# First token tiles loaded in two halves on two queues, first gate slice moved to the other queue, mask sum moved behind the prologue

## The chip, the cores and the metric

One core of one Trainium2 chip. The metric is the device time of one execution in microseconds (us). It was taken over several executions ("runs") of each kernel, with those of the kernel before interleaved on the same chip. The profiler gives a trace of one of the runs of each kernel. In its lines PE is TensorE, DVE is VectorE and ACT is ScalarE; L427 is line 427 of that kernel. A load "lands" when its last part has been reported; "pace" is the time from one matmul's start to the next.

## The reference

`x` has 2048 tokens of 512 values in bf16. It is normalised, then goes through a linear-attention block with 32 heads and through a gated block; both results are added to `x`:

```python
xn = (x - mean(x)) / sqrt(var(x) + 1e-5)
q, k, v = split(xn @ wqkv)                     # 512 x 1536
phi(t)  = concat(softmax(t @ w_phi), softmax(-t @ w_phi))
o       = phi(q) @ (phi(k).T @ v) / (phi(q) @ sum(phi(k)) + 1e-6)
out     = x + o @ wo + ((xn @ w_gate) * (xn @ w_up)) @ w_down     # 1792 wide inside
```

Only the first microseconds matter here: tokens come in 16 tiles of 128. The first four are centred, transposed on TensorE, and multiplied by the value weights `wv` (four blocks q = 0 to 3 of 128 x 512) and by the first slices of `w_gate` and `w_up`.

## The kernel before

The kernel is a list of steps with declared reads and writes. A small scheduler puts them in an order for each engine; between `sc.pin = True` and `sc.pin = False` the order is the one written. A DMA names the engine whose queue issues it: SP ("the first queue") or ACT ("the second queue"). The parts that the change touches:

```python
def load_x(t0, n, eng=SP):                       # n tiles of 128 KB
    ...
    sc.dma(eng, lambda e: e.dma_start(o, i), [], [("x", t) for t in range(t0, t0 + n)], n * 131072)

sc.pin = True
load_x(0, 1)                # first queue
load_x(1, 1, ACT)           # second queue
load_x(2, 1)
load_v(ACT, 1)              # value weights, 128 KB each
load_v(SP, 0)
load_v(ACT, 3)
load_v(SP, 2)
load_x(3, 1)
load_gu(SP, 0, (1,))        # up slice 0, 256 KB
act(sbf("lnv", 0, 1), eps_f, ["eps"], ["pace"])
load_gu(ACT, 0, (0,))       # gate slice 0, 256 KB, on the second queue
load_gu(SP, 1)              # gate and up slice 1, 384 KB each
# ... further weights and tiles on the first queue (cut)

# mask sum, early on VectorE:
dve(lambda e: e.tensor_reduce(out=epsz, in_=m1, axis=AX.XY, op=ALU.add), ["mask16"], ["epsz1"], 64)
dve(lambda e: e.tensor_scalar(out=epsz, in0=epsz, scalar1=1e-6, ...), ["epsz1"], ["epsz"], 1)
```

and the head of the pinned prologue, in the order that every engine keeps:

```python
warm(7)                       # seven matmuls of constants, 128 x 512
warm(1, 512, [("x", 0)])      # an eighth, when tile 0 has landed
sc.pin = True
ln_mean_split(0)              # half of the mean on ACT, half on VectorE
ln_mean_split(1)
ln_center_split(0)            # x - mean, in two halves of columns, on VectorE
ln_center_split(1)
x_transpose(0, 2, 0)          # PE
ln_mean_split(2)
x_transpose(0, 3, 1)
warm(1, 128)
x_transpose(1, 4, 0, DVE)
ln_center_whole(2)
x_transpose(1, 5, 1, DVE)
warm(1, 128)
for t in range(2):            # values of tiles 0 and 1 with weights q = 1, then q = 0
    v_matmul(t, t, ((1,), (0,)), stop=False)
x_transpose(2, 6, 0)
x_transpose(2, 4, 1, DVE)
for t in range(2):
    v_matmul(t, t, ((3,), (2,)), start=False)
# ... tile 3, gate and up products of slice 0 (cut)
```

The softmax here doesn't subtract the row's maximum and nothing guards it: scores larger than these inputs give would overflow.

## Time and profile before

| | before |
|---|---|
| median of the first 3 runs | 213.94 us (213.79 to 214.33) |
| span of the profiled run | 212.6 us |
| PE busy | 208.8 us, 98% |
| first transpose on PE | 4.78 us |
| PE without any stall from, to | 6.60 us, 209.7 us |

Two lines of the profile's page, the busy table and the chain of work that ended last by engine:

```profile
...
PE 208.8 (98%) x1476; PEld 125.6 (59%) x1476; DVE 165.8 (78%) x281; ACT 144.6 (68%) x350; POOL 108.8 (51%) x137
...
PE 97%; DMA 1%; DVE 1%; issue 0%
...
```

PE is the bound. A busy PE is not proof of it, since the ends of matmuls are modelled, so the starts were read as well: after 6.60 us they follow each other every 0.216 us (512 columns) or 0.109 us (256) to the last matmul. The time is therefore decided by when the prologue lets PE run freely.

The chain of waits in that prologue, in order of time (start us, us, what):

```profile
...
0.79 2.89 DMA arena<-in_A_x_dram
...
3.70 0.57 DVE arena L427 x3
...
4.38 0.08 DVE arena L427
4.46 0.27 DVE arena L434
...
4.78 0.65 PE ps L474 x4
...
6.07 1.12 PE ps L247 x4
...
```

The chain is a landing (issued at 0.79, landed at 3.68), VectorE work, then PE. VectorE's own timeline (start us, busy us, engine, line, operation, what ended the idle time before):

```profile
...
3.10 0.15 DVE L363 TENSOR_SCALAR arena<-arena 128x1 f32<-128x1 f32 x1
3.70 0.42 DVE L427 TENSOR_SCALAR_CACHE_REDUCE arena<-arena 128x256 bf16<-128x256 bf16 x1 [0.44 <-DMA arena<-in_A_x_dram]
...
4.04 0.41 DVE L427 TENSOR_SCALAR_CACHE_REDUCE arena<-arena 128x256 bf16<-128x256 bf16 x1
...
4.38 1.11 DVE L434 TENSOR_SCALAR arena<-arena 128x256 bf16<-128x256 bf16 x4
...
```

L427 are the means of tiles 0 and 1, L434 the four centring steps (two for each tile). The mask sum ends at 3.25, so VectorE sits idle for 0.44 us before tile 0 comes. Since the mean of tile 1 stands before the centring of tile 0, a late tile 1 would hold up tile 0 too. Here it does not: tile 1 landed at 3.84, while VectorE was still busy with tile 0.

PE's timeline in the same stretch:

```profile
...
4.78 0.65 PE L474 MATMUL ps<-arena 128*128 128x128 bf16 x4 [0.39 <-DVE arena L434]
...
5.33 0.63 PE L474 MATMUL ps<-arena 128*128 128x128 bf16 x4
...
5.87 1.33 PE L247 MATMUL ps<-arena 128*128 128x512 bf16 x4
7.03 0.39 PE L474 MATMUL ps<-arena 128*128 128x128 bf16 x4
...
```

L474 are the transposes, L247 the products. The first group of four 512-column products takes 1.33 us because PE still runs at half pace: their starts are 0.427 us apart until 6.3 us.

### The profile page before, as it was taken

The page shows a single profiled execution, that of the slowest core. Times are in us where ns is not written, and L with a number is a line of the kernel's source. Part 1 is how long each engine was busy: PE and PEld are TensorE (multiplying, and loading weights), DVE is VectorE, ACT ScalarE, POOL GpSimd, SP SyncE. Part 2 cuts the span into 40 slices and gives each one's busy share as a digit, 9 for nine tenths or more (in the row PEclk, how much of TensorE's full clock was granted, in tenths as well). Part 3 has the DMA queues.
Part 4 walks back from the last instruction along what each step waited for, and adds up shares of the span by engine and source line. Part 5 has one row for each costly group of instructions (what it writes and reads, how often), then busy time and mean ns, then how long its engine had stood idle before and what let it go on. Part 6 is the DMA issues. An engine that isn't in the chain of part 4 may idle for free.

```text
span 212.6 us, 4047 instructions
## 1 busy us (share of the span) xinstructions
PE 208.8 (98%) x1476; PEld 125.6 (59%) x1476; DVE 165.8 (78%) x281; ACT 144.6 (68%) x350; POOL 108.8 (51%) x137
## 2 busy tenths in 40 slices
PE   7999999999999999999999999999999999999995
PEld 2665444444554444444444444456888898899884
DVE  3686699998986647758989989896888898897622
ACT  4459998885989999987878977564544444432220
POOL 4030393243312448998895472204658549558540
DMA  5999119479500320331321223414265836556511
GB/s 166 305 283 372 65 35 187 89 200 328 104 3 0 49 49 3 60 59 33 72 53 26 49 52 49 104 54 65 48 80 131 190 70 135 125 128 148 123 49 49
DMA packets 49252, 22.29 MB, mean 105 GB/s; under 512 B 38097, under 2 KB 47697, under 8 KB 49233
## 3 DMA queue, kind: packets, MB, share of 16 engines
q1 hardware_dynamic: 48272, 21.39, 43.4%
q10 hardware_dynamic: 960, 0.66, 1.0%
q8 instruction: 11, 0.18, 0.4%
q14 instruction: 9, 0.07, 0.1%
HBM read 11.03 MB, written 2.10 MB: 62 GB/s over the span
## 4 chain that ended last, share of the span: by engine, by line
PE 97%; DMA 1%; DVE 1%; issue 0%
PE ps L247 91%; PE ps L553 2%; PE ps L611 2%; DMA arena<-in_A_x_dram 1%; PE ps L381 1%; PE ps L474 1%; DVE arena L427 0%; DVE arena L924 0%; DVE arena L434 0%; PE ps L1001 0%
## 5 line engine op out<-in xcount | busy, mean ns | idle before, releaser
L247 PE MATMUL ps<-arena 128*128 128x512 bf16 (+2 forms) x1160 | 200.0, 330 | 0.0
L247 PEld LDWEIGHTS ps<-arena 128*128 128x128 bf16 (+1 forms) x1160 | 110.9, 98 | 73.4 <-ACT arena L228 0.3
L228 ACT ACTIVATE arena<-ps 128x512 bf16<-128x512 f32 (+3 forms) x117 | 59.3, 538 | 17.9 <-PE ps L247 12.4
L228 ACT ACTIVATE arena<-arena 128x32 f32<-128x32 f32 (+8 forms) x131 | 52.4, 424 | 6.0 <-DVE arena L894 3.0
L894 DVE TENSOR_TENSOR arena<-ps,arena 128x512 f16<-128x512 f32 (+1 forms) x56 | 38.3, 685 | 19.5 <-ACT arena L228 14.2
L516 POOL TENSOR_TENSOR arena<-arena 128x1024 bf16<-128x1024 bf16 x16 | 31.0, 1934 | 38.0 <-ACT arena L228 38.0
L228 ACT ACTIVATE arena<-ps,arena 128x512 bf16<-128x512 f32 (+1 forms) x55 | 35.5, 671 | 10.1 <-PE ps L247 10.0
L506 DVE TENSOR_REDUCE arena<-arena 128x64 f32<-128x1024 bf16 x32 | 38.6, 1210 | 3.3 <-ACT arena L228 3.3
L855 POOL TENSOR_TENSOR arena<-arena 128x256 f16<-128x256 f16 x32 | 24.3, 768 | 13.0 <-DMA arena<-arena 11.7
L228 ACT ACTIVATE ps<-ps 128x256 f32<-128x256 f32 x24 | 8.8, 368 | 29.0 <-PE ps L247 29.0
L833 DVE TENSOR_TENSOR arena<-arena 128x896 f16<-128x896 f16 x32 | 23.7, 749 | 3.2 <-PE ps L247 3.1
L924 DVE SCALAR_TENSOR_TENSOR arena<-ps,arena 128x256 bf16<-128x256 f32 (+1 forms) x24 | 13.5, 569 | 10.4 <-PE ps L247 10.0
L773 POOL TENSOR_TENSOR arena<-arena 128x512 f16<-128x512 bf16 x14 | 16.2, 1175 | 4.7 <-DVE arena L894 3.3
L959 POOL TENSOR_TENSOR arena<-arena 128x512 f32<-128x512 f32 x8 | 9.5, 1192 | 17.1 <-ACT arena L228 17.1
L522 POOL TENSOR_TENSOR arena<-arena 128x512 bf16<-128x512 bf16 x16 | 17.2, 1074 | 0.9
L621 DVE TENSOR_TENSOR arena<-ps,arena 128x512 f16<-128x512 f32 x16 | 11.0, 687 | 1.4
L405 DVE BATCH_NORM_STATS2 arena<-arena 128x6 f32<-128x512 bf16 x16 | 10.4, 672 | 0.4 <-DMA arena<-in_A_x_dram 0.4
L520 POOL TENSOR_TENSOR arena<-arena 128x32 f32<-128x32 f32 x16 | 4.2, 266 | 9.5 <-ACT arena L228 9.5
L668 DVE BATCH_NORM_STATS2 arena<-arena 128x6 f32<-128x512 bf16 x14 | 9.0, 681 | 0.0
L553 PEld LDWEIGHTS ps<-arena 128*128 128x128 bf16 x128 | 6.0, 97 | 3.5
L802 DVE TENSOR_TENSOR arena<-arena 128x1792 f16<-128x1792 f16 (+1 forms) x8 | 7.0, 903 | 0.0
L611 PEld LDWEIGHTS ps<-arena 128*128 128x128 bf16 x128 | 6.2, 97 | 1.2
(54 smaller groups left out, 68.1 us busy)
## 6 DMA issues: line engine op xcount, KB each, us to landing
arena<-in_A_x_dram SPq DMA_DIRECT2D x8, 256.0 KB, 3.3
out_dram<-arena SPq DMA_DIRECT2D x15, 128.0 KB, 2.0
arena<-in_B_w_down_dram SPq DMA_DIRECT2D x1, 1792.0 KB, 7.9
arena<-in_A_x_dram SPq DMA_DIRECT2D x3, 512.0 KB, 4.2
arena<-arena SPq DMA_TRANSPOSE x44, 3.0
arena<-in_B_w_gate_dram SPq DMA_DIRECT2D x1, 640.0 KB, 8.7
arena<-in_B_w_up_dram SPq DMA_DIRECT2D x1, 640.0 KB, 9.9
arena<-in_B_w_gate_dram SPq DMA_DIRECT2D x1, 512.0 KB, 5.3
```

The lines of the kernel that those rows point to most:

```text
L228: return sc.step(ACT, lambda e: e.activation(out=out_ap, in_=in_ap, func=func, scale=scale, **kw), reads, writes, 130.0 + 0.833 * n)
L247: ins = e.matmul(out_ap, lhsT=l, rhs=r, start=start and i == 0, stop=stop and i == npair - 1, **kw)
L506: dve(lambda e: e.tensor_reduce(out=sm, in_=e_v, axis=AX.X, op=ALU.add), [(name, s, 0), (name, s, 1)], [("sums", sr)], 1024)
L516: pool(lambda e: e.tensor_tensor(out=e_w, in0=e_w, in1=r_w, op=ALU.mult), [(name, s, 0), (name, s, 1), ("rs", n)], [(name, s, 0), (name, s ...
L522: pool(lambda e: e.tensor_tensor(out=e_v[:, :, 1, :], in0=e_v[:, :, 1, :], in1=rat[:, :, None].to_broadcast([128, H, 16]), op=ALU.mult), [ ...
L611: ins = e.matmul(bank(b0 + c // 4, (c % 4) * CW, CW), lhsT=ph[:, c, :], rhs=kvz_v[:, c, :], start=True, stop=True)
L621: dve(lambda e: e.tensor_tensor(out=o_tile(t).rearrange("p (b h f) -> p b h f", b=2, f=16), in0=nd[:, :, :, 0:16], in1=w_v[:, r].unsqueeze ...
L773: pool(lambda e, ft=ft: e.tensor_tensor(out=hH_v[:, ft, 0:512], in0=hT_v[:, ft, 0:512], in1=r2w, op=ALU.mult), [("hT", ft, 0), "r2w", ("x" ...
L833: dve(lambda e, k=k, i0=i0, i1=i1, op=op: e.tensor_tensor(out=s_block(p, k), in0=i0, in1=i1, op=op), ks + more, [s_key(p, k)] + over.get(k ...
L855: pool(lambda e, k=k, i0=i0, i1=i1, op=op: e.tensor_tensor(out=so_block(p, k), in0=i0, in1=i1, op=op), ks + [("so", p, m) for m in more], ...
L894: dve(lambda e: e.tensor_tensor(out=h_v[:, ft, sg * 512:(sg + 1) * 512], in0=bank(bu), in1=g, op=ALU.mult), [("ps", bu), ("g", s)] + ([("j ...
L924: dve(lambda e: e.scalar_tensor_tensor(out=o, in0=src, scalar=inv, in1=resid, op0=ALU.mult, op1=ALU.add), keys + [rkey, "inv"], [("ostg", ...
```

## The change

The intent: tiles 0 and 1 should land earlier by having both queues carry half of each (64 of 128 partitions); to make room on the second queue the first gate slice goes to the first queue; the mask sum leaves VectorE's way; and products with value weight q = 0 come after both of q = 1, since that weight may now be later.

```diff
+    def load_x_half(t, h, eng):
+        p = slice(h * 64, h * 64 + 64)
+        o, i = x_tile(t)[p, :], rows(x_flat, t, 1)[p, 0, :]
+        sc.dma(eng, lambda e: e.dma_start(o, i), [], [("x", t) if h else ("x", t, 0)], 65536)
@@
-    load_x(0, 1)
-    load_x(1, 1, ACT)
+    for t in range(2):
+        load_x_half(t, 0, SP)
+        load_x_half(t, 1, ACT)
     load_x(2, 1)
     load_v(ACT, 1)
     load_v(SP, 0)
     load_v(ACT, 3)
     load_v(SP, 2)
     load_x(3, 1)
+    act(sbf("lnv", 0, 1), eps_f, ["eps"], ["pace"])
+    load_gu(SP, 0, (0,))
     load_gu(SP, 0, (1,))
-    act(sbf("lnv", 0, 1), eps_f, ["eps"], ["pace"])
-    load_gu(ACT, 0, (0,))
     load_gu(SP, 1)
@@ the two dve(...) of the mask sum become a function eps_z(), called after u1a(), at the end of the pinned part
@@ ln_mean_split waits for both halves of tiles 0 and 1
-    for t in range(2):
-        v_matmul(t, t, ((1,), (0,)), stop=False)
+    for q in (1, 0):
+        for t in range(2):
+            v_matmul(t, t, ((q,),), start=q == 1, stop=False)
```

## The prediction

> **What bounds the kernel now.** TensorE: 208.8 us busy of a 212.6 us span, and 97% of the chain of waits. In PE's timeline the first real work, the transposes of tile 0, starts at 4.78 us; from 6.60 us to the last matmul at 209.7 us the starts show no stall (0.216 us for 512 columns, 0.109 for 256). So the time is the moment the prologue hands over, plus a fixed amount of matmuls, plus a tail of 3 us. Only what happens before 6.6 us can be won; later only a new stall can lose.
>
> **The prologue's chain.** Tile 0 is issued at 0.79 and lands at 3.68 us; VectorE takes its mean (3.70), then, in fixed order, tile 1's mean (4.04, 0.41 us; tile 1 landed at 3.84), then centres tile 0 (4.46); PE starts at 4.78. The transposes of tiles 0 and 1 start at most 0.1 us after VectorE ends; from 5.87 us on every wait of PE has 0.25 us of slack or more for long after.
>
> **The change, costed.**
> - *Halves.* The same 256 KB, now four issues of about 0.40 us, two per queue. Tile 0 needs both halves. Packets: tile 0's first starts at 1.82; those of the second queue (tile 1) at 2.23, when the first engines have done their eight 1 KB packets of tile 0 (46 ns each). The Trainium skill (DMA: Bandwidth & Descriptors, Rules for kernel authors) says of two disjoint partition halves "Don't bother — they serialize", on the same 16 engines; these packets agree. Tile 0 may still land a little earlier, as tile 1 competes less. Estimate: tile 0 at 3.4 to 3.7, tile 1, now second on each queue, at 3.75 to 4.1. VectorE takes tile 1's mean before it centres tile 0, so tile 1 then ends the wait: centring at 4.2 to 4.55 against 4.46, so -0.25 to +0.1 us.
> - *Mask sum moved.* 0.37 us of VectorE, ending at 3.25, before tile 0 lands: no gain unless tiles land before 3.25.
> - *First gate slice on the first queue.* It landed at 7.43 and now follows tile 3: estimate 7.8, up slice 8.5; PE needs them at 8.98 and 9.64. Later issues slip 0.95 us: transposed weights 13.5 instead of 12.6, needed at 15.29. Tiles 4 to 7 land about 16.0 instead of 15.0; VectorE now takes them one gate product later. No PE stall.
> - *Order of the value products.* The wait that it relaxes had 0.57 us of slack: nothing.
>
> **Clock.** 512-column matmuls start every 0.427 us until 6.3 and every 0.216 after 6.6. The skill (TensorE: Matmul & The Clock Gate, Part 1) says that the gate follows a free-running window of about 3.4 us, so the moment varies from run to run; one profile cannot show that. An earlier start at half clock brings half its lead.
>
> **Prediction.** About 0.2 us less: 213.7 us, with 213.2 to 214.3 holding 8 in 10. Faster by over 2%: 1%; within 2%: 98%; slower by over 2%: 1%.
>
> **Signs.** Right if tile 1's landing starts the second mean, PE's first transpose starts between 4.5 and 4.9, and PE has no stall after 7 us. Wrong if both tiles land by 3.3 (a gain of 0.4 us or more), if tile 1 lands after 4.2 (a loss), or if PE stalls at 9 to 10 (gate slice), 15.3 (folded weights) or 17 to 20 us (VectorE waiting for tiles 4 to 7).

## The result, and the profile after

| | before | after |
|---|---|---|
| median, runs | 214.13 us, 6 runs (213.76 to 214.85) | 214.22 us, 6 runs (214.15 to 214.34) |
| ratio after / before | | 1.000, 95% interval 0.998 to 1.002 |
| tile 0 complete | 3.68 us | 3.47 us (halves at 3.11 and 3.47) |
| tile 1 complete | 3.84 us | 4.07 us (halves at 3.75 and 4.07) |
| first transpose on PE | 4.78 us | 4.83 us |
| value weight q = 1 / q = 0 landed | 5.04 / 5.72 us | 5.86 / 6.12 us |
| gate slice 0 landed | 7.43 us | 8.20 us |

Ratios are computed as the mean time of one kernel's runs over that of the other's of the same rounds, so they are not quite the ratio of the medians. Landings are read from the trace's semaphore events. The time is the same. But the six runs after lie within 0.2 us, and the six before within 1.1 us. That difference turned out to be the clue.

The page after, the lines that answer to those above (the busy table, the chain by engine):

```profile
...
PE 208.5 (98%) x1476; PEld 125.4 (59%) x1476; DVE 165.8 (78%) x281; ACT 144.6 (68%) x350; POOL 108.9 (51%) x137
...
PE 96%; DMA 1%; DVE 0%; ACT 0%; issue 0%
...
```

The chain of waits of the prologue after:

```profile
...
1.43 2.64 DMA arena<-in_A_x_dram
...
4.43 0.08 DVE arena L437
4.52 0.27 DVE arena L444
...
4.83 0.54 PE ps L484 x4
...
6.00 1.02 PE ps L247 x4
...
```

It now runs through a landing that was issued at 1.43 us, the second issue of the second queue: the second half of tile 1. VectorE's timeline after (L437 the means, L444 the centring):

```profile
...
3.49 0.42 DVE L437 TENSOR_SCALAR_CACHE_REDUCE arena<-arena 128x256 bf16<-128x256 bf16 x1 [3.49 <-DMA arena<-in_A_x_dram]
...
4.09 0.42 DVE L437 TENSOR_SCALAR_CACHE_REDUCE arena<-arena 128x256 bf16<-128x256 bf16 x1 [0.17 <-DMA arena<-in_A_x_dram]
...
4.43 1.11 DVE L444 TENSOR_SCALAR arena<-arena 128x256 bf16<-128x256 bf16 x4
...
```

Tile 0 came 0.21 us earlier than in the profile before, but VectorE then waited 0.17 us for tile 1 and started the centring within 0.05 us of the time before. PE's timeline after (L484 transposes):

```profile
...
4.83 0.54 PE L484 MATMUL ps<-arena 128*128 128x128 bf16 x4 [0.44 <-DVE arena L444]
...
5.34 0.54 PE L484 MATMUL ps<-arena 128*128 128x128 bf16 x4
...
6.00 1.02 PE L247 MATMUL ps<-arena 128*128 128x512 bf16 x4
6.86 0.39 PE L484 MATMUL ps<-arena 128*128 128x128 bf16 x4
...
```

Here PE ran at full pace from about 5.1 us, where the profile before had half pace until 6.3 us. PE waits before 6.00: the starts of the last short warm-up matmul and of the first product are 0.27 us apart, 0.22 us too many, and the value weight q = 1 landed at 5.86. After that there is no stall.

So one pair of profiles shows four offsetting things (tile 0 earlier, tile 1 later, a value weight later, a better clock) and a total of nothing. Experiments have to say which belong to the change.

### The profile page after: what moved, and what is told of

Its sections match the earlier page's. It is cut to its first block, busy times and chain, and to the rows that moved or that the text cites. A ratio compares the mean times of both kernels' runs of the same rounds, so it can differ in the third digit from the quotient of the medians.

```text
span 212.4 us, 4054 instructions
## 1 busy us (share of the span) xinstructions
PE 208.5 (98%) x1476; PEld 125.4 (59%) x1476; DVE 165.8 (78%) x281; ACT 144.6 (68%) x350; POOL 108.9 (51%) x137
## 4 chain that ended last, share of the span: by engine, by line
PE 96%; DMA 1%; DVE 0%; ACT 0%; issue 0%
PE ps L247 91%; PE ps L563 2%; PE ps L621 2%; DMA arena<-in_A_x_dram 1%; PE ps L390 1%; PE ps L484 1%; ACT L1205 0%; DVE arena L934 0%; DVE arena L444 0%; DVE arena L437 0%; PE ps L1011 0%
```

## The experiments

The first theory was that of the prediction: tile 1's landing ends the wait, the rest of the change is off the critical path, and the clock's moment varies by chance. Its rival: the parts of the change have real effects that cancel. There were twelve runs: nine new kernels and three repeats (before_again, after_again, rest_again). All were correct. "Whole" below means tiles 0 and 1 loaded whole.

### Only the halves

```diff
# kernel before, plus:
-    load_x(0, 1)
-    load_x(1, 1, ACT)
+    for t in range(2):
+        load_x_half(t, 0, SP)
+        load_x_half(t, 1, ACT)
```

> Only the halves; gate slice, mask sum and product order as before. Theory (the landing of tile 1 ends the wait): tile 0 lands near 3.5 us and tile 1 near 4.05, PE's first transpose starts at 4.75 to 4.9, as in both kernels; time within 0.3 us of before. Rival (the halves gain and the other parts of the change give it back): PE's first transpose at 4.5 or earlier and the time 0.3 us or more below before.

Measured: 214.43 us (214.28 to 214.55), ratio 0.999 (0.998 to 1.001). Tile 0 landed at 3.42, tile 1 at 4.06, and PE's first transpose started at 5.00. VectorE:

```profile
...
3.44 0.42 DVE L434 TENSOR_SCALAR_CACHE_REDUCE arena<-arena 128x256 bf16<-128x256 bf16 x1 [0.19 <-DMA arena<-in_A_x_dram]
...
4.08 0.42 DVE L434 TENSOR_SCALAR_CACHE_REDUCE arena<-arena 128x256 bf16<-128x256 bf16 x1 [0.21 <-DMA arena<-in_A_x_dram]
...
4.60 1.12 DVE L441 TENSOR_SCALAR arena<-arena 128x256 bf16<-128x256 bf16 x4
...
```

The halves bring PE nothing: tile 1, the second issue on each queue, ends the wait of the second mean, as expected, and the first transpose is even later than expected (5.00 against 4.75 to 4.9). Two things here do not come from tile 1's landing. ScalarE issues the gate slice's DMA from 3.45 to 3.87, and its half of tile 0's mean starts after that, at 3.98, though the tile landed at 3.42 (in the profile after it starts at 3.55); centring starts at 4.60 against 4.43 after, with tile 1 landing at the same time. And tile 3 lands at 8.43, so that PE stalls by 0.33 us before its transposes. Lines from the timelines of ACT and PE:

```profile
...
3.98 0.42 ACT L228 ACTIVATE arena<-arena 128x256 bf16<-128x256 bf16 x1 [0.34 <-issue]
...
9.53 0.40 PE L481 MATMUL ps<-arena 128*128 128x128 bf16 x4 [0.17 <-DVE arena L446]
...
```

None of the six runs reached the 214.7 to 215.0 of the slow runs of before; the gate slice, still on the second queue, is issued at 3.45 here instead of 2.24.

### The change without the halves

```diff
# changed kernel, with:
-    for t in range(2):
-        load_x_half(t, 0, SP)
-        load_x_half(t, 1, ACT)
+    load_x(0, 1)
+    load_x(1, 1, ACT)
```

> The change without the halves: tiles 0 and 1 whole, one on each queue; gate slice on the first queue, mask sum late, new product order. Theory: tile 0 lands near 3.68 and tile 1 near 3.84 as before, PE's first transpose at 4.78 as before; the first value weight lands near 5.0 again instead of 5.86, so no PE stall of 0.2 us near 6.0; time within 0.3 us of before. Rival (the other parts cost what the halves win): a PE stall after 7 us and the time 0.3 us or more above before.

Measured: 213.86 us (213.81 to 214.02) beside 214.74 (213.75 to 214.97) of the kernel before; ratio 0.9969 (0.9951 to 0.9988). Tile 0 landed at 3.43, tile 1 at 3.60, the first transpose started at 4.54. PE:

```profile
...
4.54 0.54 PE L483 MATMUL ps<-arena 128*128 128x128 bf16 x4
...
5.48 1.18 PE L247 MATMUL ps<-arena 128*128 128x512 bf16 x4
...
```

Both theories missed: the parts that were priced at nothing make the kernel 0.3% faster, clear of noise, and take away the whole upper half of the spread. So the change holds a gain and a loss.

### Which part gains: gate slice, mask sum, product order, one at a time

```diff
# gate_only: kernel before, with
-    load_gu(SP, 0, (1,))
     act(sbf("lnv", 0, 1), eps_f, ["eps"], ["pace"])
-    load_gu(ACT, 0, (0,))
+    load_gu(SP, 0, (0,))
+    load_gu(SP, 0, (1,))
# sum_only: kernel before, with eps_z() called behind u1a() as in the change
# order_only: kernel before, with the new loop over q and t
# before_again: kernel before, unchanged
```

> The kernel before against itself, to size what chance does. Its runs so far go from 213.75 to 214.97 us. Theory (two things vary from run to run, the landing of tiles 0 and 1 by some 0.2 us and the moment of the clock): the same spread of about 1 us here, ratio within 0.998 to 1.002, and a clock moment in the profile that differs from 6.5 us. Rival (the earlier spread came from the other kernels beside it): all runs within 0.3 us of each other.

> The kernel before with only the first gate slice moved to the first queue. Theory A (this move is what made the change without the halves fast, because the second queue then carries nothing beside the tiles but two weights): 213.8 to 214.0 us in nearly every run. Theory B (it is off the critical path, PE having over 0.5 us of slack there): same times and same spread as the kernel before; gate slice lands near 7.7 us.

> The kernel before with only the mask sum moved behind the prologue. Theory A (VectorE waits for the mask from GpSimd before it may take the first mean, and in some runs the mask is later than the tile): 213.8 to 214.0 us in nearly every run, the upper half of the spread of the kernel before gone. Theory B (the sum ended at 3.25, before the tile landed at 3.68, so it costs nothing): same times and spread as the kernel before.

> The kernel before with only the new order of the value products, so that PE asks for the second value weight one product later (0.22 us). Theory (PE's wait for the late second value weight makes the upper group of times): the upper group stays but comes down by about 0.2 us, median 214.3 to 214.6 beside 214.65 of before, best runs unchanged near 213.8. Rival (the order removes the wait altogether): all runs 213.7 to 214.0.

| kernel | median us (range) | ratio to before, 95% |
|---|---|---|
| before_again | 214.64 (214.03 to 214.94) | 0.9997 (0.998 to 1.002) |
| gate_only | 213.81 (213.69 to 214.29) | 0.9968 (0.9953 to 0.9983) |
| sum_only | 214.42 (213.68 to 214.98) | 0.9991 (0.997 to 1.001) |
| order_only | 214.34 (214.12 to 214.53) | 1.0001 (0.998 to 1.002) |

The move of the gate slice alone gives the gain. The mask sum is worth nothing that these runs can see. The kernel before against itself keeps its spread, so the spread belongs to it. The profile of before_again (a run of 214.70 us) shows what its slow runs can look like. PE's timeline:

```profile
...
4.60 0.65 PE L474 MATMUL ps<-arena 128*128 128x128 bf16 x4 [0.21 <-DVE arena L434]
...
5.69 0.63 PE L247 MATMUL ps<-arena 128*128 128x512 bf16 x1
6.72 0.82 PE L247 MATMUL ps<-arena 128*128 128x512 bf16 x3 [0.40 <-DMA arena<-in_A_wqkv_dram]
...
```

PE did one product with weight q = 1 at 5.69 and then had to wait until 6.72: the value weight q = 0, on the first queue, landed at 6.68 instead of 5.72. The same stretch of gate_only:

```profile
...
4.58 0.54 PE L474 MATMUL ps<-arena 128*128 128x128 bf16 x4 [0.35 <-DVE arena L434]
...
5.52 1.08 PE L247 MATMUL ps<-arena 128*128 128x512 bf16 x4
6.44 0.39 PE L474 MATMUL ps<-arena 128*128 128x128 bf16 x4
...
```

There that weight landed at 5.73 and the four products follow without the long gap (0.04 us is left of it). In order_only the weight q = 0 landed at 5.99, in time, but the next one, q = 3, only at 7.03; PE waits for it after the third tile's transposes:

```profile
...
6.51 0.39 PE L474 MATMUL ps<-arena 128*128 128x128 bf16 x4
7.16 2.32 PE L247 MATMUL ps<-arena 128*128 128x512 bf16 x12 [0.27 <-DMA arena<-in_A_wqkv_dram]
```

With the later request no run was above 214.53, while 6 of the 11 of the kernel before in the same rounds were. That is what was expected of a wait that is made shorter and not removed; that no run came below 214.12 was not expected, and six runs are too few to say more.

### Another load in the gate slice's old place

```diff
# gate_only, with gate slice 1 (384 KB) on the second queue in the old place of gate slice 0
+    load_gu(ACT, 1, (0,))
     load_gu(SP, 0, (0,))
     load_gu(SP, 0, (1,))
-    load_gu(SP, 1)
+    load_gu(SP, 1, (1,))
```

> The kernel with the first gate slice on the first queue, but with another load in its old place on the second queue: the second gate slice (384 KB), which PE needs only after 13 us. Theory (whatever large load stands third on the second queue shares each transfer engine with the second value weight, on which PE waits near 5.9): the second queue moves 60 to 75 KB per 0.25 us from 5.5 us on while the first falls below 25; the second value weight lands anywhere from 5.7 to 6.7, and runs spread over 214.3 to 215.2 us; the first gate slice, slower too, may stall PE near 8.5. Rival (it is the gate slice's own arrival that mattered, earlier or safer on the first queue): 213.7 to 214.0 us.

Measured: 214.90 us (214.26 to 216.63), ratio 1.003 (1.000 to 1.007); the profiled run took 215.40. The value weight q = 0 landed at 6.90 and the first gate slice at 9.84. PE:

```profile
...
5.66 0.38 PE L247 MATMUL ps<-arena 128*128 128x512 bf16 x1
6.95 0.82 PE L247 MATMUL ps<-arena 128*128 128x512 bf16 x3 [0.91 <-DMA arena<-in_A_wqkv_dram]
...
```

The wait came back, longer (a stall of 1.07 us), and with the late gate slice a second stall of 0.33 us came near 9.9. So it is not the gate slice's own arrival that mattered. A large load behind tile 1 and two value weights on the second queue can make loads of the first queue late. It does not do so every time: of the six profiles with such a load there and whole tiles, the weight q = 0 landed at 6.68 and 6.90 in two and at 5.60 to 5.99 in four. One run, of 216.63 us, was slower than any theory had said; it was not profiled. What each queue moved, counted from the trace's packets, in KB for each 0.25 us:

```
from us                5.00  5.25  5.50  5.75  6.00  6.25
before        first      53    51    22    13    30    61
              second     27    28    54    65    55    27
before_again  first      45    38    24    22    49    60
              second     28    38    62    64    41    25
other_on_act  first      54    35    17    12    11    30
              second     24    35    60    76    79    54
gate_only     first      57    70    71    75    73    77
              second     23     9     1     2     0     0
```

The second queue's large load takes the transfer engines just when the first queue has the weights and tile 3 to bring. But this is not the whole mechanism: in the profile before the queues shared in the same way, and there the weight q = 0 landed in time, at 5.72. What differs is a tail. In before_again 12 of the 16 increments of that weight's semaphore had come by 5.45 us, and the other four between 5.89 and 6.68; on the second queue weight q = 3, which stands ahead of the gate slice there, had 12 by 5.62 and the other four from 6.15 to 6.92. A few parts of both loads came up to 1.2 us behind the rest. Why stays open: the trace does not name the engine of a packet.

### How the loss of the halves grows

```diff
# changed kernel, tiles 0 and 1 in quarters of 32 partitions
+    for t in range(2):
+        load_x_quarter(t, 0, SP)
+        load_x_quarter(t, 1, ACT)
+        load_x_quarter(t, 2, SP)
+        load_x_quarter(t, 3, ACT)
```

> The changed kernel with tiles 0 and 1 in four quarters each, two per queue and tile: the suspected cost, issues on the way of tile 1, doubled at the same bytes. Theory (each issue holds its queue for 0.4 to 0.6 us, so tile 1 comes later with each further issue): the last quarter of tile 1 is the fourth issue of its queue, begins near 2.3 to 2.9 and lands at 4.7 to 5.4; PE's first transpose at 5.4 to 6.2; time 0.4 to 1.2 us above before. Rival (bytes on the 16 engines decide, issues are free): tile 1 lands by 4.2, PE's first transpose by 5.0, time within 0.3 us of before.

Measured: 214.51 us, with a range of 214.32 to 216.15, ratio 1.001 (0.998 to 1.004). The last quarter landed at 4.16, PE's first transpose started at 4.93. My expectation fell and the rival's held: doubling the issues did not make tile 1 later (halves: 4.06 to 4.34). Two of the six runs, 215.00 and 216.15, stand above all runs of the kernel before; the first is the profiled one, with PE stalls of 0.37 us near 6.3 (weight q = 1) and 0.36 us near 10.3. The issues themselves explain part: 0.41 to 0.44 us each here, 0.40 for whole tiles, but 0.57 to 0.84 for the four issues of halves (in all four profiles with halves: 0.58, 0.57, 0.57 and 0.84 to within 0.01 us, then 0.58 and 0.61 for the two issues behind them, though these are loads of all 128 partitions). Why issues take longer in the kernels with halves is open; the shape of the load alone does not explain it. What both splits do share is that everything behind them starts later: the value weight q = 1 is issued at 1.25 with whole tiles, 2.30 with halves and 2.67 with quarters, and lands at 5.04, 5.86 and 6.14; PE's first product starts at 5.87, 6.00 and 6.27.

### Centring tile 0 before the mean of tile 1

```diff
# changed kernel, with
     ln_mean_split(0)
-    ln_mean_split(1)
     ln_center_split(0)
+    ln_mean_split(1)
     ln_center_split(1)
```

> The changed kernel, with VectorE told to centre tile 0 before it takes the mean of tile 1. Theory (tile 1's landing at 4.07 held back tile 0 only through VectorE's fixed order): tile 0 is centred at about 3.95 and PE's first transpose starts near 4.3 instead of 4.83; the transposes of tile 1 start near 5.3 to 5.5, no earlier than before, so the time falls by at most 0.2 us. Rival (tile 0's own landing is what ends the wait): the first transpose stays at 4.8.

Measured: 214.32 us (214.29 to 214.42), ratio 0.999 (0.997 to 1.000). VectorE:

```profile
...
3.60 0.42 DVE L437 TENSOR_SCALAR_CACHE_REDUCE arena<-arena 128x256 bf16<-128x256 bf16 x1 [3.60 <-DMA arena<-in_A_x_dram]
...
4.22 0.60 DVE L444 TENSOR_SCALAR arena<-arena 128x256 bf16<-128x256 bf16 x2 [0.19 <-ACT arena L228]
4.73 0.41 DVE L437 TENSOR_SCALAR_CACHE_REDUCE arena<-arena 128x256 bf16<-128x256 bf16 x1
...
5.19 0.60 DVE L444 TENSOR_SCALAR arena<-arena 128x256 bf16<-128x256 bf16 x2
...
```

Tile 0 is centred from 4.22, before tile 1 had even landed (4.26), so its hold through VectorE's order is shown; the wait is now for ACT's half of the mean. The first transpose started at 4.62, later than the 4.3 expected. Tile 1's transposes started at 5.59 instead of 5.34, and the time did not fall. PE's next products need both tiles, and tile 1's mean now waits behind the centring (4.73), so freeing tile 0 alone bought nothing here.

### The clock

```diff
# kernel before, without
-    warm(7)
-    warm(1, 512, [("x", 0)])
```

> The kernel before without its eight warm-up matmuls. Theory (the clock follows what PE did in a window before, and its moment is what spreads the times): PE's first transpose at 4.78 still, matmuls at half pace (0.427 us per 512 columns) until somewhere from 8 to 12 us, time 1.2 to 2.8 us above before. Rival (the clock opens at a fixed time whatever PE does): full pace from about 5 to 6.6 us as in the two profiles, time within 0.3 us of before.

Measured: 215.93 us (215.43 to 216.75), ratio 1.007 (1.004 to 1.010). PE:

```profile
...
4.63 0.65 PE L474 MATMUL ps<-arena 128*128 128x128 bf16 x4 [4.63 <-DVE arena L434]
...
5.71 1.91 PE L247 MATMUL ps<-arena 128*128 128x512 bf16 x4
...
```

Transposes start as before, but half pace lasts until about 8.8 us (the four products take 1.91 us instead of 1.33). The clock follows what PE did earlier, as the Trainium skill says (TensorE: Matmul & The Clock Gate, Part 1). And its moment does vary by chance: in the profiles of kernels that open PE with the same eight warm-up matmuls, full pace begins at about 3.6 us (the kernel with the other centring order: its seventh and eighth warm-up matmuls start 0.34 us apart instead of 0.427), before 4.7 (gate_only), at about 4.8 (the change without the halves), 5.1 (after), 5.8 (halves only), 6.0 (rest_again, below) and 6.5 (before). Two profiles of one and the same kernel, the change without the halves, gave 4.8 and 6.0. So the better clock of the first profile after is not shown to be the change's.

### The changed kernel and the change without the halves, again on one chip

> The changed kernel again, on the same chip as the next run. Theory (moving the gate slice wins about 0.7 us against the mean of before, the halves give back about 0.4): 214.1 to 214.4 us; tile 1 lands at 3.95 to 4.15 and the first value weight at 5.7 to 5.9 in the profile; issues on the two queues 0.57 to 0.84 us. Chance alone would give 213.8 to 215.

> The change without the halves again, the version that should beat both kernels. Theory: 213.75 to 214.05 us in every run, 0.3 to 0.4 us below the changed kernel of the same rounds and 0.4 to 0.8 us below before; tile 1 lands at 3.6 to 3.85, the first value weight near 5.0, the second near 5.8, no PE stall over 0.2 us after 5 us. Rival (its first result was chance): runs up to 214.9 as the kernel before has.

Measured in the same rounds: the changed kernel 214.27 us (214.16 to 214.37), the change without the halves 214.04 (213.95 to 214.10), the kernel before 214.58 (213.77 to 214.80). Ratios to before: 0.9996 (0.998 to 1.002) and 0.9986 (0.9968 to 1.0004). The version without the halves is 0.23 us below the changed kernel, a little less than expected, and all of its runs are below all of the changed kernel's. Its interval against before touches 1 in these rounds; in the first it did not. PE's timeline of its profiled run:

```profile
...
4.78 0.65 PE L483 MATMUL ps<-arena 128*128 128x128 bf16 x4 [0.39 <-DVE arena L443]
...
5.86 1.09 PE L247 MATMUL ps<-arena 128*128 128x512 bf16 x4
...
```

In this run tile 0 landed at 3.67 and tile 1 at 3.83, as in the profile before, and full pace came only at about 6.0 us. The weights were in time (q = 1 at 5.03, q = 0 at 5.98) and nothing stalled. The run took 214.10 us against 213.83 of this kernel's first profile, where tile 0 landed 0.24 us earlier and full pace came at about 4.8: so a late clock and late tiles together cost some 0.3 us here, not the 0.8 us or so between the two groups of the kernel before. The changed kernel's profile here had tile 1 at 4.34, beyond the 4.15 expected, and its first transpose at 5.11.

## Why the prediction was right or wrong

**The total fell inside the range, by luck: "About 0.2 us less: 213.7 us, with 213.2 to 214.3".** Measured 214.22 us, no change within 0.2%, and near the range's upper end. Two of its terms were wrong and cancelled: the halves lost where a small gain was expected, and the gate slice's move, priced at nothing, gained.

**What bounds the kernel: right.** In all fourteen profiles the stretch from PE's first matmul of the weight folding that follows the prologue (L381 before; it starts between 14.69 and 16.37 us; 15.29 before, 15.11 after) to its last matmul takes 194.41 us, to within 0.01. So every difference between these profiled runs is made before that stretch, in the prologue.

**The halves, "-0.25 to +0.1 us": mis-sized.** The step to tile 1 was right ("tile 1, now second on each queue ... then ends the wait"), and so were the first profile's landings: 3.47 in 3.4 to 3.7, 4.07 in 3.75 to 4.1. Two things were off. The four issues were priced at "about 0.40 us" and took 0.57 to 0.84. And the base was one profile in which the whole tiles landed rather late (3.68, 3.84): in the eight profiles of whole tiles with the warm-up matmuls (both of before, gate_only, sum_only, order_only, other_on_act, both without halves), the first transpose started at 4.54 to 4.78, on average 4.64. In three with halves (both of after, and halves alone) it started at 4.83, 5.00 and 5.11, on average 4.98. That is a loss of 0.34 us in PE's start (in halves alone, part of it is ScalarE's late mean). In time: 12 runs of the changed kernel average 214.25 us, 12 runs of it without the halves 213.96, so 0.29 us. In the kernel before the halves cost nothing that shows (0.9994): there they also put off the gate slice's issue from 2.24 to 3.45, and none of those runs reached the slow group. The parts do not simply add. The skill's advice on two disjoint partition halves (DMA: Bandwidth & Descriptors, Rules for kernel authors: "Don't bother — they serialize") agrees with the traces: in the four profiles with halves the two halves of a tile landed 0.31 to 0.56 us apart. It would have been better read as a cost than as a zero.

**"First gate slice on the first queue ... No PE stall": true, and it missed the point.** The slice lands later (8.20) and PE does not stall for it. But the step asked only when PE needs the moved load, not what the load did to others where it was. The one profile had 0.57 us of slack at the value weight q = 0 and I took that for a property of the kernel. It was a property of that run. The move alone is worth 0.3% (0.9968, 0.9953 to 0.9983). Over all rounds, 27 of 45 runs of the kernel before took more than 214.5 us, and none of 36 runs of four versions with the gate slice on the first queue did (gate_only, the change without and with the halves, and the changed kernel with the other centring order). The kernel with quarters, which also has the slice there, did in 3 of 6 runs; so keeping the second queue free of large loads is not enough there. The late value weight explains the one run of the upper group that was profiled (before_again), and other_on_act brought such a wait about; that it makes the whole group is inferred, since unprofiled runs show their time only.

**"Order of the value products ... nothing": right for the time, within noise.** Alone it neither gains nor loses on average; it seems to shorten the wait when that weight is late.

**"Mask sum moved ... no gain": right** (0.9991, 0.997 to 1.001).

**"Clock": right that it varies by chance.** When full pace begins was seen to vary by about 3 us (3.6 to 6.5).

**The signs.** First transpose between 4.5 and 4.9: yes in the first profile (4.83), no in the second (5.11). No PE stall after 7 us: yes. The one sign that fired against me, "if tile 1 lands after 4.2 (a loss)", did so in the second profile (4.34).

The sum, from the averages of all rounds (these mix rounds, so read them as sizes only): before 214.46 us over 45 runs; minus 0.50 us for the change without the halves, nearly all of it the gate slice's move; plus 0.29 us for the halves on top; after 214.25 us over 12 runs. Both terms are differences of these averages, so that they add up proves nothing. The best version that came of it is the change without the halves, or the gate slice's move alone: 213.96 and 213.88 us on average.

## What to carry to other kernels

When a load is moved between queues, look for gain or loss in the loads that it no longer shares time with, above all the one that the bottleneck waits for next, and not only at the moved load's own deadline. A slack read from one profile is one draw: before trusting a few tenths of a microsecond, look at the spread of the times, because a wide or two-humped spread says that some wait is only sometimes there. And a change of several parts with a total of nothing should be taken apart, since here a part worth keeping was hidden behind one worth undoing.

## What the Trainium skill lacked or had wrong

- DMA: Bandwidth & Descriptors, on issuing from several engines (section "Issuing engines are not separate DMA queues": it "will only save the time on the sequencer"): here the choice of queue did more. Moving one 256 KB load to the other queue was worth 0.3% (ratio 0.9968), and with a large load behind two value weights on the second queue a weight on the first landed at 6.68 and 6.90 us in two of six profiles, instead of 5.60 to 5.99. The page describes elsewhere how an engine serves several queues, but not what this does to the landing of small loads.
- The same page has no figure for the issue time of such small loads from two queues at once. The runs show 0.39 to 0.46 us in the kernels with whole tiles (128 partitions), 0.41 to 0.44 for quarters (32), and 0.57 to 0.84 for halves (64); but the two loads of 128 partitions right behind the halves took 0.58 and 0.61 us, so the shape is not shown to be the cause.
- TensorE: Matmul & The Clock Gate, Part 1: it gives the change of pace as around 4 us into sustained activity, give or take 0.5 us. Here, counted from the first matmul at 0.82 us, it came after about 2.8 us (the kernel with the other centring order) to about 5.7 us (before), with short idle times in between. The page does not say how much idle time the busy window may hold; in the changed kernel's profile full pace began at 5.1 us although PE had sat idle for 0.44 us before 4.83.
